# A new order for the head of a fused attention and MLP kernel: mask rows and query low part first, values by slot, adjacent banks, and 91 matmuls of a constant

## The chip, the cores and the metric

The kernel runs on one core of a Trainium2 chip. The metric is the device time of one execution in microseconds, as the median of several runs; lower is better.

## What is computed

Attention with a block-sparse mask, followed by a gated MLP. There are 4 batches, 8 heads, 768 positions of 64 values; the mask works on blocks of 32 positions, with three random blocks a row that come as an input.

```python
scores = scale * np.matmul(q, k.transpose(0, 1, 3, 2))
# mask: neighbours, first and last block row and column, and for each qb the blocks sampled_blocks[qb]
scores = np.where(mask, scores, -1000000000.0)
scores = scores - np.max(scores, axis=-1, keepdims=True)
attn = np.exp(scores)
attn = attn / (np.sum(attn, axis=-1, keepdims=True) + 1e-09)
x = np.matmul(attn, v).transpose(0, 2, 1, 3).reshape(B * S, H * D)   # 3072 x 512
h = x @ w_in                                                          # 512 -> 2048
return (h * np.clip(h + 3.0, 0.0, 6.0) / 6.0) @ w_out                 # 2048 -> 512
```

## The kernel before

The attention is cut into 64 units of one batch, one half of the query positions (384) and one head, u0 to u63. The MLP is cut into 64 steps, m0 to m63: for each batch and half, eight steps of 256 hidden columns. The 32 weight blocks w0 to w31 come as 64-bit floats; ACT (`size`) and DVE (`bits_0` to `bits_2`, `low`) turn each into a high and a low part of 32 bits. The mask is prepared once (k0).

All instructions are issued in an order that is written out by hand: a string, SCORE, names one step after another (`u0 s_0` is the first score pair of unit 0). A step that is named early does first what it needs. Each engine works through its own queue in that order, and so does SP, which issues every load and store.

A unit goes through these steps. `loadq`, `loadk`, `loadv` load; `qh` and `kh` round query and key on ACT; `ql` writes the query's low part on DVE, `kl` the key's on POOL; `qb` copies the query below the mask rows. `m_0` to `m_2` are matmuls for the row maxima, two of 384 columns each, `r_0` to `r_2` the maxima over blocks of 32 on DVE, `fin` adds the block mask `mq` and takes the maximum. `mt` turns it by a matmul with the unit matrix (units 0 to 9) or by a DMA (from 10 on), `qm` copies it into the row of `qb` on ACT. `s_0` to `s_2` are the scores, four matmuls each (`QA,KA` and `qb,kb`), `e_0` to `e_2` the exps on ACT, `av` the product with the values. `uc`, `dw` or `tt`, `uu` empty it; `rg`, `rc`, `rs`, `rb` spread the denominators over partitions by DMA and back; `ux` scales. The MLP's `h_` matmuls need the scaled heads of half a row of units, `ga` to `gl` are the gate, `o_` the second product.

PSUM has eight banks: two tiles `big` of two banks, one `av`, and three single tiles `out0` to `out2` for the MLP's result. Units 1 to 8, which come before the MLP starts, use two of the `out` banks for their maxima, in turn. Units 0 to 11 are wide: their value tile holds, for each of six chunks, 64 columns of values and 64 of ones. The later ones use the two 64-column parts as two slots.

Of the kernel before, what the change touches and what calls it, by code (L numbers as in the profile page):

```python
# [20 lines left out]
P = 128  # L21
# [21 lines left out]
    ql; w2 size; k0 kb_0; u0 m_0; u1 loadq; w0 size; u0 m_1 r_0; k0 indc; u0 r_1 m_2; k0 kb_1; u0 kl r_2; k0 rows mq
    qb_11; u1 qh; w2 bits_0; u1 loadk qb; w2 bits_1; k0 qb_01 identc mqc qb_10; u0 fin_0 fin_1; k0 qb_00; w2 bits_2;
    u0 mt qm; w0 bits_0; w1 load; w2 high; u0 s_0; w0 bits_1; u0 s_1; w2 low; u0 e_0; u1 ql; w2 save; u0 e_1 s_2; w0
    bits_2; u2 loadq; u0 av_0; u1 kh; w3 load; w0 high; u1 kl m_0; u0 e_2 av_1; u1 r_0; w1 size; w0 low; u2 loadk; u1
    m_1; u0 av_2; w1 bits_0; u2 qh; w0 save; w1 bits_1; u2 qb ql; w3 size; u2 loadv; w1 bits_2; u3 loadq; u0 dw; u1
    r_1; w5 load; w1 high; u0 uc; w1 low; u1 m_2; u2 kh; u1 r_2; w1 save; u2 kl m_0 r_0; u3 loadk; u1 fin_0; u2 m_1;
    w5 size; u1 fin_1; w3 bits_0; u1 mt; u2 r_1; u1 qm s_0; w5 bits_0; u1 s_1 e_0; w5 bits_1; u2 m_2; w5 bits_2; u1
    e_1 s_2; u2 r_2; w4 load; u1 av_0; w5 high; u1 e_2; u2 fin_0 fin_1; u1 av_1; w5 low; u3 kh; w3 bits_1; w5 save; u3  # L50
    qh; u1 av_2; w3 bits_2; u3 qb ql; w3 high; w6 load; u2 mt; u3 kl; u4 loadq; u3 m_0; u1 dw; u3 loadv r_0; u2 qm; u1
    uc; u2 s_0; w4 size; u1 rg; w3 low; u2 s_1 e_0; u4 loadk; w4 bits_0; u3 m_1; w3 save; w4 bits_1; u2 e_1; m1
    loadout_0; u2 s_2; u3 r_1; u2 av_0; w6 size; u2 e_2; w6 bits_0; w4 bits_2; u3 m_2; u4 qh; u2 av_1; u3 r_2; w8
    load; w4 high; u4 qb; u2 av_2; u1 rc; u4 ql; u1 rs; u4 kh; u3 fin_0; u5 loadq; u3 fin_1; u4 kl m_0; u2 dw; u4
    loadv; u3 mt; u4 r_0; u3 qm; u2 uc; u3 s_0; w6 bits_1; u5 loadk; u3 s_1; w8 size; w6 bits_2; u4 m_1; u3 e_0; w8
    bits_0; w7 load; u1 rb; u4 r_1; w6 high; u3 s_2 e_1 av_0; w6 low; u3 e_2; w4 low; w6 save; u4 m_2; u5 qh; w8
    bits_1; w4 save; u3 av_1; u5 kh ql; u4 r_2; u5 qb; u6 loadq; u5 kl; u3 av_2; w7 size; u5 m_0; u3 dw; u5 loadv r_0;
    u6 loadk; u3 uc rg; u1 ux_0; u5 m_1; m1 loadin_0; u4 fin_0; u1 ux_1; u4 fin_1; m1 loadin_1; u5 r_1; u4 mt qm s_0;
    u1 ux_2; w8 bits_2; u4 s_1 e_0; w7 bits_0; w10 load; u5 m_2; w8 high; w7 bits_1; u4 s_2 e_1; u3 rc; u4 av_0; u5
    r_2; u3 rs; u6 kh; u5 fin_0; u4 av_1; u5 fin_1; u4 e_2; u6 kl qh; u4 av_2; u6 qb; w10 size; u6 ql; u7 loadk; u5  # L60
    mt; w7 bits_2; u7 loadq; u6 m_0; u4 dw; u5 qm; u6 r_0; w9 load; u6 loadv; w7 high; u5 s_0; u3 rb; w8 low; u4 uc;
    u5 s_1 e_0; w7 low; w8 save; u6 m_1; u5 e_1 s_2; w10 bits_0; w7 save; u6 r_1; u5 av_0 e_2; w10 bits_1; u7 kh; u6
    m_2; w10 bits_2; u5 av_1; u7 qh; u6 r_2; u7 kl; w11 load; w10 high; u5 av_2; u7 qb; m1 loadout_1; w9 size; u3
    ux_0; u8 loadk; u5 uc; u7 loadv; u6 fin_0 fin_1; u3 ux_1; u7 ql; u6 mt; u5 dw; u3 ux_2; u7 m_0; u8 loadq; u6 qm;
    u5 rg; w9 bits_0; u6 s_0; w11 size; u7 r_0; u6 s_1 e_0; w9 bits_1; u7 m_1; u6 e_1 s_2; w9 bits_2; u6 av_0; u7 r_1;
    w12 load; w9 high; u6 e_2; w9 low; u7 m_2; u8 kh; u6 av_1; u5 rc; w9 save; u7 r_2; u5 rs; u8 qh kl qb; u6 av_2; u7
    fin_0; u6 uc; u8 loadv; u7 fin_1; u8 ql; u9 loadk; u7 mt; u6 dw; w10 low; u8 m_0; u9 loadq; u7 qm; w12 size; u7
    s_0; u8 r_0; u5 rb; u7 s_1 e_0; w12 bits_0; w10 save; u8 m_1; w11 bits_0; u7 e_1 s_2; w11 bits_1; u7 av_0; u8 r_1;
    u7 e_2; u9 kh; w11 bits_2; u8 m_2; u7 av_1; w12 bits_1; w14 load; w11 high; u8 r_2; u9 kl qh; u7 av_2; u9 qb; u8
    fin_0; u7 uc; u9 loadv; u8 fin_1; u10 loadk; u5 ux_0; u8 mt; u7 dw; u9 ql; u8 qm; u7 rg; w12 bits_2; u5 ux_1; u9  # L70
    m_0; u10 loadq; u8 s_0; w14 size; u5 ux_2; w13 load; w12 high; u9 r_0; u8 e_0; w14 bits_0; u8 s_1; w14 bits_1; u8
    s_2 e_1; w14 bits_2; u8 av_0 e_2; w11 low; w15 load; u7 rc; w14 high; w12 low; u7 rs; u9 m_1; w11 save; u9 m_2;
    u10 kh; u9 r_1; w12 save; u8 av_1; u10 qh kl; u9 r_2; u10 qb; u8 av_2; w13 size; u9 fin_0 fin_1; u8 uc; u10 loadv;
    w14 low; u9 mt; u8 dw; u7 rb; w13 bits_0; u9 qm; w13 bits_1; w14 save; w15 size; u9 s_0; u11 loadk; w13 bits_2; u9
    s_1 e_0; w15 bits_0; w16 load; u10 ql; w13 high; u9 s_2; w15 bits_1; u11 loadq; u9 e_1 av_0; w13 low; u9 e_2; w15
    bits_2; w13 save; u9 av_1; u7 ux_0; w15 high; w18 load; u7 ux_1; w15 low; u10 m_0; u11 kh; u10 m_1; u7 ux_2; w15
    save; u9 av_2; u10 r_0; u11 qh kl qb; u10 r_1 m_2; w16 size; u11 loadv; u9 uc; u10 r_2; m0 h_00; u12 loadk; u9 dw;
    w18 size; u9 rg; w16 bits_0; m0 h_10; u10 fin_0 fin_1; w18 bits_0; u10 mt; m0 h_01; w16 bits_1 bits_2; m0 h_11; m2
    loadin_0; w18 bits_1; w16 high; w17 load; m1 h_00; w18 bits_2; m0 ga; m2 loadin_1; u11 ql; w19 load; m1 h_10; w18
    high; u9 rc; u12 loadq; m0 gb; u9 rs; m1 h_01; w18 low; m0 gh; w16 low; w18 save; u10 s_0; m3 loadin_0; m0 gl; w16  # L80
    save; w17 size; m1 h_11; u10 e_0; m3 loadin_1; w19 size; u10 s_1; w17 bits_0; u9 rb; m1 ga; w17 bits_1; m0 o_00;
    w19 bits_0; m0 o_01; u10 e_1; w17 bits_2; m0 o_10; w19 bits_1; w17 high; w20 load; u10 s_2; w19 bits_2; m0 o_20;
    u10 e_2; w17 low; w22 load; u10 av_0; m2 loadout_0; m1 gb; w19 high; w17 save; u12 kh; u9 ux_0; u11 m_0 m_1; u12
    qh; w19 low; m0 o_11; u9 ux_1; u11 r_0; u12 kl; w19 save; m0 o_21; u12 qb; m1 gh; u10 av_1; u11 r_1; m2 loadout_1;
    w22 size; m1 gl; u13 loadk; u11 m_2; w20 size; u10 av_2; u11 r_2; u9 ux_2; m2 h_00; u10 uc; u12 loadv; w22 bits_0;
    u14 loadv; u10 dw; u11 fin_0; m2 h_10; u11 fin_1; w22 bits_1; u11 mt; w22 bits_2; m2 h_01; u12 ql; w22 high; w24
    load; m2 h_11; w20 bits_0; u13 loadq; m4 loadin_0; w22 low; u12 m_0; w20 bits_1; w22 save; m2 ga; m1 o_00; m4
    loadin_1; u12 r_0; m1 o_01; m2 gb; m1 o_10; u12 m_1; w20 bits_2; m2 gh; u12 m_2; m1 o_20; u12 r_1; w21 load; w20
    high; m2 gl; m1 o_11; m3 loadout_0; w24 size; u12 r_2; u11 s_0; m1 o_21; w24 bits_0; u11 e_0; u12 fin_0; u11 s_1;
    u12 fin_1; m3 loadout_1; w24 bits_1; u12 mt; u11 s_2 e_1; w24 bits_2; u11 av_0 e_2; w20 low; w23 load; w20 save;  # L90
    w24 high; m2 o_00; u13 kh; w24 low; m2 o_01; w24 save; u13 qh kl; u12 s_0; u13 qb; u12 s_1; w21 size; u11 av_1;
    u12 e_0; u13 ql; u14 loadk; u12 e_1; w21 bits_0; u14 loadq; u13 m_0; w21 bits_1; u11 av_2; w23 size; u13 r_0 m_1;
    w23 bits_0; u11 uc; u13 loadv m_2; u12 suma; u15 loadv; u11 dw; m2 o_10; u11 rg; m2 o_20; u13 r_1; m2 o_11; m4
    loadout_0; u13 r_2; u12 s_2; u13 fin_0; m3 h_00; u13 fin_1; u12 e_2; w23 bits_1; u13 mt; w23 bits_2; u14 kh; m3
    h_10; u12 sumb; w26 load; w23 high; u12 av; u14 qh; u11 rc; u14 kl; u11 rs; u14 qb; u13 s_0; u12 tt sumc; u15
    loadk; u16 loadv; m3 h_01; u12 uu; u13 e_0; u14 ql; u13 s_1; w26 size; w23 low; u15 loadq; m5 loadin_0; m3 h_11;
# [826 lines left out]
```

## Time and profile before

| | before |
|---|---|
| median of 3 runs | 998.83 us (998.39 to 999.71) |
| the profiled execution | 998.31 us, span 996.5 us |
| PE busy | 954.3 us, 96% of the span |
| DVE, ACT, POOL busy | 649.4, 468.2, 248.8 us |
| mean granted clock of PE | 0.990 |
| DMA | 155.48 MB in 136981 packets, 72755 of them under 512 B |

PE carries the span, so its gaps and its clock are read first, stage by stage. A row of the stage table gives a stretch, each engine's busy time in it with the count of its instructions, the granted clock, the share of the DMA engines and the rate. A row in order of time gives start, duration, engine, line, operation and tiles, and in brackets how long the engine was idle before it and what ended that. Since nearly all instructions go through one helper, their line says nothing; the tile names do.

### The profile page before, as it was taken

The page shows a single profiled execution, that of the slowest core. Times are in us where ns is not written, and L with a number is a line of the kernel's source. Part 1 is how long each engine was busy: PE and PEld are TensorE (multiplying, and loading weights), DVE is VectorE, ACT ScalarE, POOL GpSimd, SP SyncE. Part 2 cuts the span into 40 slices and gives each one's busy share as a digit, 9 for nine tenths or more (in the row PEclk, how much of TensorE's full clock was granted, in tenths as well). Part 3 has the DMA queues.
Part 4 walks back from the last instruction along what each step waited for, and adds up shares of the span by engine and source line. Part 5 has one row for each costly group of instructions (what it writes and reads, how often), then busy time and mean ns, then how long its engine had stood idle before and what let it go on. Part 6 is the DMA issues. An engine that isn't in the chain of part 4 may idle for free.

```text
span 996.5 us, 13217 instructions
## 1 busy us (share of the span) xinstructions
PE 954.3 (96%) x4750; PEld 772.0 (77%) x4750; DVE 649.4 (65%) x924; ACT 468.2 (47%) x712; POOL 248.8 (25%) x148
## 2 busy tenths in 40 slices
PE   5888889999999999999999999999999999999998
...
PEclk9799799999999999999999999999999999999999
...
GB/s 183 188 224 210 222 264 217 216 224 182 149 153 138 136 121 172 149 132 140 162 139 132 96 165 158 136 126 154 159 114 140 128 149 183 103 78 141 161 122 74
DMA packets 136981, 155.48 MB, mean 156 GB/s; under 512 B 72755, under 2 KB 85171, under 8 KB 136916
## 3 DMA queue, kind: packets, MB, share of 16 engines
...
q8 instruction: 37, 0.61, 0.3%
...
## 4 chain that ended last, share of the span: by engine, by line
PE 83%; DVE 6%; ACT 4%; issue 3%; DMA 3%; POOL 0%; SPq 0%; DVEq 0%; ACTq 0%; POOLq 0%
PE big L356 46%; PE out L356 24%; PE av L356 13%; DVE acc L356 2%; DVE bm L356 2%; DMA wraw<-w_out 1%; ACT pr L356 1%; ACT qb L356 1%; DMA wout_lo<-xhl 1%; DVE xhl L356 1%; DVE QA L356 1%; ACT rec L356 0%; DMA qb<-mneg 0%; ACT g L356 0%; DMA spread<-rec 0%
## 5 line engine op out<-in xcount | busy, mean ns | idle before, releaser
L356 PE MATMUL big<-xhl,win_hi 128*128 128x384 f32 x1024 | 264.0, 339 | 2.7 <-DVE bm L356 2.1
L356 POOL TENSOR_TENSOR glo<-g,ghi 128x768 fp32r<-128x768 f32 x64 | 118.7, 1855 | 477.2 <-ACT ghi L356 456.8
L356 DVE TENSOR_REDUCE bm<-big 128x24 f32<-128x768 f32 x168 | 158.6, 954 | 82.0 <-PE big L356 80.8
L356 ACT ACTIVATE pr<-big 128x768 f32<-128x768 f32 x192 | 152.0, 812 | 123.6 <-PE big L356 123.0
L356 PEld LDWEIGHTS big<-xhl,win_hi 128*128 128x128 f32 x1024 | 185.5, 188 | 14.5 <-DVE bm L356 6.0
L356 POOL TENSOR_TENSOR kb<-kraw,KA 64x768 fp32r<-64x768 f32 x64 | 124.7, 1948 | 254.5 <-ACT KA L356 208.2
L356 PE MATMUL big<-xhl,wlo_in 128*128 128x384 f32 x512 | 173.1, 338 | 0.0
L356 PE MATMUL av<-pr,vo 128*64 128x384 f32 (+1 forms) x768 | 166.1, 498 | 0.0
L356 PE MATMUL out<-wout_hi,ghi 128*128 128x512 f32 x384 | 152.8, 398 | 0.0
L356 PE MATMUL out<-wout_hi,glo 128*128 128x512 f32 x384 | 151.7, 395 | 0.0
L356 PE MATMUL out<-wlo_out,ghi 128*128 128x512 f32 x384 | 150.7, 392 | 0.0
L356 PE MATMUL big<-QA,KA 128*128 128x384 f32 x384 | 139.3, 363 | 5.9 <-ACT pr L356 2.8
L356 PE MATMUL big<-qb,kb 97*128 97x384 f32 x384 | 135.0, 352 | 8.9 <-ACT qb L356 7.7
L356 ACT ACTIVATE g<-big,half_b 128x768 f32<-128x768 f32 x64 | 57.7, 902 | 159.7 <-PE big L356 145.9
L356 DVE SCALAR_TENSOR_TENSOR g<-g,big 128x768 f32<-128x768 f32 x64 | 60.8, 949 | 95.1 <-ACT g L356 94.8
L356 PEld LDWEIGHTS av<-pr,vo 128*64 128x64 f32 (+1 forms) x768 | 69.2, 149 | 65.6 <-issue 50.9
L356 PE MATMUL big<-KA,QA 128*128 128x384 f32 x336 | 93.8, 370 | 12.5 <-DVE QA L356 10.4
L356 DVE TENSOR_TENSOR acc<-pr 128x768 f32<-128x768 f32 x52 | 57.9, 1113 | 69.3 <-ACT pr L356 69.2
L356 PEld LDWEIGHTS big<-KA,QA 128*128 128x128 f32 x336 | 75.6, 255 | 33.6 <-issue 13.3
L356 PEld LDWEIGHTS big<-xhl,wlo_in 128*128 128x128 f32 x512 | 96.1, 188 | 0.3 <-DMA wlo_in<-win_lo 0.3
L356 PEld LDWEIGHTS big<-QA,KA 128*128 128x128 f32 x384 | 74.9, 195 | 27.2 <-ACT pr L356 8.4
L356 ACT CAST ghi<-g 128x768 fp32r<-128x768 f32 x64 | 53.3, 833 | 79.4 <-DVE g L356 54.0
...
## 6 DMA issues: line engine op xcount, KB each, us to landing
...
```

What stands on the lines that cost most here:

```text
L356: return lambda *a, **k: tc.keep_in_program_order(op(*a, **k))
```

## The change

Five things. First, the opening: query and key of unit 0 are loaded first, the mask's rows `krows` (tile `pr`) and the unit matrix ahead of the first weights; the query's low part is computed ahead of the mask; the mask's step `allow` is cut into four; the block mask `mq` is multiplied from the plain F32 copy of `krows`.

Second, the two value slots lie behind each other (slot, chunk, column) from unit 12 on, where they were interleaved (chunk, slot, column).

Third, the three `out` banks are one tile OUT. The early maxima always use its first two banks, and one reduce reads both.

Fourth, `warm` steps: a tile of ones is filled on POOL as the first thing, and 91 matmuls of 384 columns multiply it with itself into the third bank of OUT. Nothing reads their result. SCORE has them at 21 places between the opening and unit 9's maxima; the last digit of the name is the count.

Fifth, SCORE has a new order up to the first MLP steps, and some exchanges of neighbours in stretches behind them.

```diff
+    OUT = outp.tile([P, NT, DM], F32, name="out")
-    VO = [const.tile([P, NC, 2, D], F32, name=f"vo{side}") for side in range(2)]
+    VO = [const.tile([P, 2 * NC * D], F32, name=f"vo{side}") for side in range(2)]
...
+        def heat(self):
+            self.hot = sb.tile([P, 2, HALF], F32R, name="ghi")
+            nc.gpsimd.memset(self.hot.bitcast(F32), 1.0)
+
+        def warm(self, *number):
+            for _ in range(number[-1]):
+                pe.matmul(OUT[:, 2, :HALF], lhsT=self.hot[:, 0, :P], rhs=self.hot[:, 1], start=True, stop=True)
...
         def mq(self):
-            self.mqp = big_tile()
+            self.mqp = OUT[:, 2]
             for t in range(NC):
-                pe.matmul(self.mqp[:, 0, t * NB:(t + 1) * NB], lhsT=self.ind_r[...], rhs=self.mval[:, 64:88], start=True, stop=True)
+                pe.matmul(self.mqp[:, t * NB:(t + 1) * NB], lhsT=self.ind_f[...], rhs=self.mval[:, 64:88].bitcast(F32), start=True, stop=True)
...
         def loadv(self):
-            self.vo = VO[self.side]
-            self.vv = self.vo[:, :, self.side if self.wide else self.n // 2 % 2]
+            if self.wide:
+                self.vo = VO[self.side].rearrange("p (c a d) -> p c a d", a=2, d=D)
+                self.vv = self.vo[:, :, self.side]
+            else:
+                self.vv = VO[self.side].rearrange("p (a c d) -> p a c d", a=2, d=D)[:, self.n // 2 % 2]
...
         def m(self, t):
             if self.early:
-                bank = (self.n - 1) // 2
-                ps = [outp.tile([P, DM], F32, name=f"out{(bank + 1 + j) % NT}")[:, :HALF] for j in range(2)]
+                ps = OUT[:, 0:2]
...
         def r(self, t):
-            if self.early:
-                for j in range(2):
-                    dve.tensor_reduce(out=bm[:, j], in_=self.mps[t][j].rearrange("p (n e) -> p n e", e=BLK), axis=AX.X, op=ALU.max)
-            else:
-                dve.tensor_reduce(out=bm, in_=self.mps[t].rearrange("p j (n e) -> p j n e", e=BLK), axis=AX.X, op=ALU.max)
+            dve.tensor_reduce(out=bm, in_=self.mps[t].rearrange("p j (n e) -> p j n e", e=BLK), axis=AX.X, op=ALU.max)
...
-    k0 samp; u0 loadq loadk; k0 table; w0 load; w2 load; k0 ind index; u0 loadv; u1 loadv; k0 ident allow; u0 qh qb kh
+    u0 loadq loadk; k0 samp table ind; u1 loadv; k0 ident; u0 loadv; w0 load; w2 load; u0 qh qb ql kh; k0 index; u1
```

What stands in the queues now, at three places. First SP's opening, the loads in their order (`samp` and `tab` are the mask's inputs, `wraw` a weight block), before:

```order
L356 DMA samp<-sampled 24x6
L356 DMA qraw<-qT 128x384
L356 DMA kraw<-kT 128x768
L356 DMA tab<-table 24x48
L356 DMA wraw<-w_in 128x1024 x2
L356 DMA pr<-krows 33x768
L356 DMA vo_119<-vP 128x6x64
L356 DMA vo_120<-vP 128x6x64
L356 DMA tmp<-ident 128x128
```

and now:

```order
L358 DMA qraw<-qT 128x384
L358 DMA kraw<-kT 128x768
L358 DMA samp<-sampled 24x6
L358 DMA tab<-table 24x48
L358 DMA pr<-krows 33x768
L358 DMA vo_121<-vP 128x6x64
L358 DMA tmp<-ident 128x128
L358 DMA vo_120<-vP 128x6x64
L358 DMA wraw<-w_in 128x1024 x2
```

The query and key went to the top, and the two weight loads moved behind five others.

Second, DVE from the mask's last row to unit 0's `fin` (`bm<-bm,mq`), before:

```order
L356 TENSOR_SCALAR mval<-tab 24x24
L356 SCALAR_TENSOR_TENSOR QA<-qraw,QA 64x384
L356 TENSOR_REDUCE bm<-big 128x24 x3
L356 TENSOR_SCALAR xhl<-xhl 128x512
L356 SCALAR_TENSOR_TENSOR xhl<-wraw,xhl 128x512
L356 COPY mq<-big 128x144
L356 TENSOR_TENSOR bm<-bm,mq 128x72
```

and now:

```order
L358 TENSOR_SCALAR mval<-tab 24x24
L358 TENSOR_REDUCE bm<-big 128x24 x2
L358 COPY mq<-out 128x144
L358 TENSOR_REDUCE bm<-big 128x24
L358 TENSOR_SCALAR xhl<-xhl 128x512
L358 SCALAR_TENSOR_TENSOR xhl<-wraw,xhl 128x512
L358 TENSOR_TENSOR bm<-bm,mq 128x72
```

The low part (`QA<-qraw,QA`) has left this place; it is now DVE's first instruction. The two weight steps stay ahead of `fin`.

Third, PE from the first product of values of unit 7 to unit 8's first scores, before (`big<-ident,mneg` is unit 8's `mt`, `big<-KA,QA` unit 9's maxima):

```order
L356 MATMUL av<-pr,vo_120 128x384 x2
L356 MATMUL out_911<-KA,QA 128x384
L356 MATMUL out_912<-KA,QA 128x384
L356 MATMUL av<-pr,vo_120 128x384 x4
L356 MATMUL big<-ident,mneg_117 2x128 x3
L356 MATMUL big<-KA,QA 128x384 x2
L356 MATMUL big<-QA,KA 128x384
```

and now, from unit 8's last maximum on (`out<-ghi` are the constants):

```order
L358 MATMUL out<-KA,QA 128x384 x2
L358 MATMUL big<-KA,QA 128x384 x4
L358 MATMUL out<-ghi 128x384 x2
L358 MATMUL big<-KA,QA 128x384 x2
L358 MATMUL out<-ghi 128x384 x16
L358 MATMUL big<-ident,mneg_117 2x128 x3
L358 MATMUL out<-ghi 128x384
L358 MATMUL big<-QA,KA 128x384
```

All three maxima of unit 9 and 19 constants stand ahead of unit 8's scores now, where it was one maximum.

More of the change, by code (lines that the diff above doesn't have):

```diff
@@ L41 @@
 SCORE = """
-    k0 samp; u0 loadq loadk; k0 table; w0 load; w2 load; k0 ind index; u0 loadv; u1 loadv; k0 ident allow; u0 qh qb kh
[L43 to L96, printed above, removed]
@@ new lines @@
+    r_1; k0 warm_101; u1 s_0; w5 bits_1; u1 s_1 e_0; w5 bits_2; u2 m_2; u1 e_1 s_2; w3 bits_2; w4 load; u2 r_2; u1
+    av_0; w5 high; w6 load; u1 e_2; u2 fin_0 fin_1; u1 av_1; w5 low; u3 kh; w5 save; u3 qh kl; u1 av_2; u3 qb; w3
+    high; u2 mt; u1 dw; u3 loadv ql; u4 loadk; u2 qm; w3 low; k0 warm_111; u3 m_0; u4 loadq; u1 uc; u2 s_0; u3 r_0; w3
+    save; w4 size; u1 rg; u2 s_1 e_0; w4 bits_0; m1 loadout_0; u3 m_1; w4 bits_1; u2 e_1 s_2; u3 r_1; u2 av_0; w6
+    size; w4 bits_2; u2 e_2; w6 bits_0; u3 m_2; w8 load; u4 qh; u2 av_1; w6 bits_1; w4 high; u3 r_2; u4 qb; u2 av_2;
@@ new lines @@
+    e_0; u1 ux_2; u5 m_2; w8 bits_2; u4 e_1 s_2; w7 bits_0; w10 load; u4 av_0; w8 high; w7 bits_1; u4 e_2; u5 r_2; u4
+    av_1; u6 qh; u3 rc; u6 qb; u5 fin_0; u3 rs; u5 fin_1; u6 kh ql; u4 av_2; w7 bits_2; u7 loadq; w8 low; w7 high; w9
+    load; u5 mt; u6 m_0 loadv; u4 dw; w7 low; w8 save; w10 size; u6 kl r_0; w7 save; u5 qm; u4 uc; k0 warm_147; u5
+    s_0; u3 rb; u5 s_1; w10 bits_0; u5 e_0; w10 bits_1; u7 loadk; u6 m_1; u5 e_1 s_2; u6 r_1; u5 av_0; w9 size; w10
+    bits_2; u5 e_2; m1 loadout_1; w9 bits_0; w11 load; u6 m_2; u7 qh; w9 bits_1; u5 av_1; w10 high; u6 r_2; u7 qb; u5
@@ new lines @@
+    av_2; u3 ux_0; u7 kh; u6 fin_0 fin_1; u7 ql; u6 mt; u5 uc; u7 loadv; w9 bits_2; u7 m_0; u8 loadq; u3 ux_1; u7 kl
+    r_0; u5 dw; w12 load; u6 qm; u5 rg; k0 warm_154; u7 m_1; w11 size; u6 s_0; u7 r_1; w9 high; u8 loadk; u6 s_1 e_0;
+    u3 ux_2; u7 m_2; w9 low; u6 e_1 s_2; u7 r_2; w9 save; u6 av_0 e_2; u7 fin_0 fin_1; u8 qh; w10 low; u6 av_1; u8 qb;
+    u5 rc; w10 save; w12 size; u8 ql; u5 rs; u6 av_2; w11 bits_0; u9 loadq; u8 kh; w12 bits_0; w11 bits_1; u7 mt; u8
+    m_0; u6 uc; u8 loadv; w11 bits_2; u6 dw; u8 kl r_0; w14 load; u7 qm; w11 high; k0 warm_164; u7 s_0 s_1 e_0; w12
@@ new lines @@
+    bits_1; u9 loadk; u8 m_1; u5 rb; u7 e_1; w12 bits_2; u7 s_2; u8 r_1; w13 load; u7 av_0; w12 high; u7 e_2; w11 low;
+    u7 av_1; u9 qh; w12 low; w11 save; u9 qb ql; w12 save; w14 size; u7 av_2; u10 loadq; w14 bits_0; u9 kh; w14
+    bits_1; u8 m_2; u9 loadv; u7 uc; u5 ux_0; u9 m_0 m_1; u7 dw; u9 kl r_0; u5 ux_1; u7 rg; w13 size; u8 r_2; k0
+    warm_172; u9 m_2; u5 ux_2; u10 loadk; u8 fin_0 fin_1; w14 bits_2; u9 r_1; w14 high; w15 load; u9 r_2; k0 warm_189
+    warm_197; u8 mt qm; k0 warm_201; u8 s_0; u7 rc; u9 fin_0; u7 rs; u9 fin_1; u8 s_1; w14 low; u8 e_0; w13 bits_0;
@@ new lines @@
+    w14 save; u8 e_1 s_2; w13 bits_1; u8 av_0; w13 bits_2; u10 kh; w16 load; u8 e_2; u10 kl; u8 av_1; u10 qh qb; u7
+    rb; u9 mt; u8 av_2; w15 size; u10 ql; u11 loadk; u9 qm; w15 bits_0; u11 loadq; w13 high; w15 bits_1; u9 s_0; u10
+    loadv; u8 uc; w13 low; u9 s_1 e_0; w15 bits_2; w13 save; u8 dw; u9 s_2; w18 load; w15 high; u9 av_0 e_1; w15 low;
+    u7 ux_0; w15 save; u9 e_2 av_1; u7 ux_1; u11 kh; u7 ux_2; u10 m_0 m_1 r_0; u9 av_2; u11 qh kl qb; u10 r_1; w16
+    size; u10 m_2; u11 loadv; u9 uc; m0 h_00; u10 r_2; u12 loadk; u9 dw; w18 size; u9 rg; w16 bits_0; m0 h_10; u10
@@ new lines @@
+    w22 load; u10 e_2; m1 gb; w17 save; m0 o_21; u12 kh; u11 m_0; w19 low; m2 loadout_1; u11 m_1; u10 av_0; u12 qh;
+    u11 r_0; w19 save; u12 kl qb; u11 r_1; m1 gh; u10 av_1; w20 size; u9 ux_0; u13 loadk; u12 ql; u11 m_2; w22 size;
+    u10 av_2; m1 gl; u13 loadq; u11 r_2; u9 ux_1; m2 h_00; u10 uc; u12 loadv; u14 loadv; w22 bits_0; u10 dw; m2 h_10;
+    w22 bits_1; u9 ux_2; m2 h_01; w22 bits_2; u11 fin_0; w22 high; w24 load; m2 h_11; u11 fin_1; m4 loadin_0; w20
+    bits_0; u11 mt; w22 low; u12 m_0; m2 ga; m4 loadin_1; w20 bits_1; m1 o_00; w22 save; u12 r_0; m1 o_01 o_10; m2 gb;
@@ new lines @@
+    u12 m_1; w20 bits_2; u12 m_2; m2 gh; m1 o_20; u12 r_1; w21 load; w20 high; m2 gl; m1 o_11; m3 loadout_0; w24 size;
+    u12 r_2; u11 s_0; m1 o_21; u11 e_0; w24 bits_0; u12 fin_0; u11 s_1; u12 fin_1; m3 loadout_1; w24 bits_1; u12 mt;
+    u11 s_2 e_1; w24 bits_2; m2 o_00; w20 low; w23 load; w24 high; m2 o_01; u11 e_2; w24 low; w20 save; u11 av_0; w24
+    save; u13 kh qh kl; u11 av_1; u13 qb; w21 size; u12 s_0; u13 ql; u14 loadk; u12 s_1 e_0; w21 bits_0; u14 loadq;
+    u11 av_2; w21 bits_1; u12 e_1; w21 bits_2; w23 size; u13 m_0; u12 suma; w26 load; u13 m_1; u11 uc; u13 loadv; m2
@@ new lines @@
+    o_10; u15 loadv; u11 dw; u13 r_0; m2 o_20; w21 high; u11 rg; w23 bits_0; u13 m_2; m4 loadout_0; u13 r_1; m2 o_11
+    o_21; u13 r_2; u12 s_2; m4 loadout_1; u13 fin_0 fin_1; m3 h_00; w23 bits_1; u12 e_2; u13 mt; w23 bits_2; u14 kh;
+    m3 h_10; u12 sumb; w28 load; w23 high; u12 av; u14 qh; u11 rc; u14 kl; u11 rs; u14 qb; w26 size; u13 s_0; u12
+    sumc; u15 loadk; u12 tt; u16 loadv; u14 ql; m3 h_01; u13 e_0; u12 uu; u15 loadq; w23 low; u13 s_1; m5 loadin_0;
+    w26 bits_0; w23 save; m3 h_11; u13 e_1; w26 bits_1; u11 rb; w26 bits_2; u13 s_2; m3 ga; m5 loadin_1; u13 suma; w30
@@ new lines @@
+    e_0; u15 fin_0 fin_1; w26 low; u15 mt; m4 o_00; u14 e_1; w26 save; u14 s_2; u11 ux_1; u14 suma; m4 o_10; u14 e_2;
+    u11 ux_2; m5 h_00; u16 kh; u14 sumb; m5 h_10; u16 qh; u14 sumc; u16 qb ql; u15 s_0; w30 size; u16 kl; u17 loadq;
+    m5 h_01; w25 size; m6 loadin_1; u15 e_0; m5 h_11; m7 loadin_0; w30 bits_0; u17 loadk; w25 bits_0; u15 s_1; m5 ga;
+    w25 bits_1; u14 av; w25 bits_2; u15 e_1; m5 gb; w27 load; w25 high low; m5 gh; u15 s_2; u18 loadv; u15 suma; u14
+    tt; w25 save; u16 m_0; u15 e_2; m4 o_20; m5 gl; u16 r_0; u17 kh; m4 o_01; u14 uu; u16 m_1; u17 qh; u16 m_2; u17
@@ L411, in fused_kernel @@
         NEEDS = {
-            "indc": "ind", "identc": "ident", "kb_0": "ind", "kb_1": "ind", "index": "samp", "allow": "index table", "mq": "allow indc", "rows": "allow indc", "mqc": "mq",
+            "index": "samp", "allow_0": "index table", "allow_1": "allow_0", "allow_2": "allow_1", "allow_3": "allow_2",
+            "mq": "allow_3 ind", "rows": "allow_3 indc", "indc": "ind", "mqc": "mq", "identc": "ident", "kb_0": "ind", "kb_1": "ind",
             "qb_00": "rows", "qb_01": "rows", "qb_10": "rows", "qb_11": "rows",
@@ L447, in index, with allow @@
             dve.tensor_copy(out=self.idxf, in_=self.sampled[:, 0:6:2])
-        def allow(self):
-            self.mval = const.tile([NB, 88], F32R, name="mval")
-            nc.gpsimd.memset(self.mval.bitcast(F32), 0.0)
+        def allow(self, j):
             msk = self.tab[:, 1]
-            for j in range(3):
+            if j == 0:
+                self.mval = const.tile([NB, 88], F32R, name="mval")
+                nc.gpsimd.memset(self.mval.bitcast(F32), 0.0)
+            if j < 3:
                 eq = sb.tile([NB, NB], F32, name="eq")
```

477 lines of the change are left out of this document (245 added, 232 removed).

## Prediction, made before the changed kernel ran

> **What bounds the kernel now.** I read first the page's slices, then one table of busy time by stage, then PE's rows of the first 140 us in order of time with what ended each gap, and last the chain of waits for the same stretch. The profiled execution took 998.31 us, a span of 996.5 and 1.8 around it; the median of the runs shown is 998.83, 0.5 above it. The sum below is made against 998.31.
>
> ```profile
> PE   5888889999999999999999999999999999999998
> PEclk9799799999999999999999999999999999999999
> ```
>
> PE is full from the seventh slice on. What is open lies in the first five or six slices, and the granted clock dips there too. The stages, with engine busy time in the order PE, PEld, DVE, ACT, POOL, then clock, DMA share and GB/s:
>
> ```profile
> 0.00:121.00 121.00, 95.38 (x345) 68.46 (x345) 91.71 (x172) 82.86 (x136) 27.85 (x32) 0.92 0.66 206
> ...
> 28.50:39.50 11.00, 8.57 (x25) 6.91 (x26) 7.73 (x18) 4.61 (x8) 1.81 (x1) 0.54 0.52 160
> 39.50:99.50 60.00, 52.44 (x217) 36.94 (x215) 51.92 (x97) 47.44 (x80) 12.85 (x7) 1.00 0.70 216
> 99.50:107.00 7.50, 6.48 (x17) 5.10 (x17) 4.27 (x9) 5.59 (x10) 1.22 (x1) 0.54 0.83 283
> ...
> 113.80:117.50 3.70, 3.70 (x9) 2.42 (x8) 3.16 (x6) 2.68 (x6) 0.00 (x0) 0.54 0.87 277
> ...
> 136.00:996.50 860.50, 846.51 (x4341) 692.02 (x4340) 546.18 (x733) 376.74 (x564) 218.95 (x115) 1.00 0.50 148
> ```
>
> The head, 0 to 121 us, ends with the first MLP matmul. In it PE is idle for 25.6 us and at about half clock for 22; behind 136 us it is busy for 98.4% and any lead won in the head is carried to the end as it stands. Inside the head no engine is full: from 39.5 to 99.5 PE and DVE have 52 of 60 us each, so units are paced by hand-overs between two nearly full queues.
>
> ```profile
> 7.56 1.62 PE L356 MATMUL big<-KA,QA 128*128 128x384 f32 x4 [7.56 <-DVE QA L356]
> ...
> 18.18 0.52 PE L356 MATMUL big<-qb,kb 97*128 97x384 f32 x1
> 18.50 0.52 PE L356 MATMUL big<-QA,KA 128*128 128x384 f32 x1
> ...
> 27.22 0.98 PE L356 MATMUL out<-KA,QA 128*128 128x384 f32 x2 [1.45 <-DVE bm L356]
> ...
> 33.89 0.66 PE L356 MATMUL big<-qb,kb 97*128 97x384 f32 x1 [1.84 <-ACT qb L356]
> ...
> 43.92 0.41 PE L356 MATMUL big<-qb,kb 97*128 97x384 f32 x1 [0.61 <-ACT qb L356]
> 44.17 0.34 PE L356 MATMUL big<-QA,KA 128*128 128x384 f32 x1
> 44.34 0.34 PE L356 MATMUL big<-qb,kb 97*128 97x384 f32 x1
> ...
> 89.98 0.41 PE L356 MATMUL big<-qb,kb 97*128 97x384 f32 x1 [0.74 <-ACT qb L356]
> ...
> 100.69 0.69 PE L356 MATMUL big<-QA,KA 128*128 128x384 f32 x1 [1.02 <-DVE bm L356]
> ...
> 111.81 0.41 PE L356 MATMUL big<-qb,kb 97*128 97x384 f32 x1 [1.52 <-ACT qb L356]
> ...
> 135.76 0.44 PE L356 MATMUL big<-QA,KA 128*128 128x384 f32 x1 [2.60 <-ACT pr L356]
> ```
>
> Three things to see. The matmuls of 384 columns start 0.32 us apart at 18 us and about 0.175 apart at 44: PE runs at half speed in its first stage too, although the clock column says 1.00 there. Unit 1 has its first scores at 33.89, 17 us behind unit 0, while units 2 to 7 follow each other by 9.2 (43.92 to 89.98, five steps). And the gaps that precede the dips are short: 1.45, 1.02 and 1.52 us.
>
> **The start.** In order of time, all engines:
>
> ```profile
> 0.75 0.43 SPq L356 DMA_DIRECT2D samp<-sampled  x1
> ...
> 1.24 0.37 SPq L356 DMA_DIRECT2D qraw<-qT  x1
> ...
> 2.56 0.81 SPq L356 DMA_DIRECT2D wraw<-w_in  x2
> ...
> 4.78 0.83 ACT L356 CAST KA<-kraw 128x768 fp32r<-128x768 f32 x1
> ...
> 6.66 0.17 DVE L356 TENSOR_SCALAR mval<-tab 24x24 fp32r<-24x24 f32 x1
> 6.86 0.56 DVE L356 SCALAR_TENSOR_TENSOR QA<-qraw,QA 64x384 fp32r<-64x384 f32 x1
> ...
> 8.58 1.82 DVE L356 TENSOR_REDUCE bm<-big 128x24 f32<-128x768 f32 x2 [1.16 <-PE big L356]
> ...
> 9.68 1.23 ACT L356 ACTIVATE xhl<-wraw 128x512 f32<-128x512 f32 x2 [4.06 <-DMA wraw<-w_in]
> ...
> 14.49 1.22 ACT L356 CAST qb<-big 24x384 fp32r<-24x384 f32 x3
> ...
> 16.01 0.67 ACT L356 CAST qb<-big 1x384 fp32r<-1x384 f32 x1 [0.30 <-PE big L356]
> ```
>
> The low part of the query now stands ahead of the mask work on DVE, and its load is issued 0.5 us earlier; the first maxima then wait for KA alone, which ends near 5.2 instead of 5.6, so they start about 2.3 us sooner. DVE reads them once the mask row (mval, end 6.83) is out: 1.7 us sooner than 8.58. Against this the two weight loads go behind krows, both values and ident, 547 KB. At the 206 GB/s of the head that is 2.6 us, at the 283 of a dense stage 1.9; I take 2.1, so the second weight lands at 11.8. Its size step (0.62) and then six ACT rows (four casts of 0.41, two of about 0.5) stand ahead of the unit's qb: 15.1 instead of 16.01. Both ways of loading leave between 0.3 and 2.3; I take **0.9**. On DVE two weight steps (0.5 and 0.7) stand between the last maximum and fin; they end near 13.5 and are hidden by that ACT row.
>
> **The clock in the first stage.** 25 constants come ahead of unit 0's mt: ten while PE would be empty until 5.2 (4 us at 0.32 each is 3.2), fifteen while it waits for the maxima (2.6 to 4.8 us in a gap of some 4). If PE is warm by then, its 12 score matmuls gain 0.14 each, **1.7**. Most of it reaches unit 1 through the exps: its first maxima and the size step of the next weight.
>
> **Unit 1.** The chain of waits has a load here:
>
> ```profile
> 27.12 5.25 DMA wraw<-w_out
> 32.40 0.66 ACT xhl L356
> 33.08 0.68 ACT qb L356
> ```
>
> The load needs a buffer that DVE frees with the last bit step of weight 1. Before, that step stands behind unit 2's low part; now the three bit steps stand together right behind unit 1's first maximum. With exps 0.9 + 1.7 earlier less what ACT's casts take up (KA, win_hi in between; I walk the rows to a size step 1.3 sooner), the step ends near 23.8, 2.9 before the load's 27.12. ACT still waits for that load ahead of unit 1's qb, so the 2.9 goes through one for one: unit 1's scores at 31.0. So start and clock together are worth **2.9** here, not 0.9 + 1.7. Twelve score matmuls of unit 1 without the dip of 28.5 give again **1.7**.
>
> **Early maxima.** 48 reduces of half a bank pair become 24 of both:
>
> ```profile
> L356 DVE TENSOR_REDUCE bm<-big 128x24 f32<-128x768 f32 x168 | 158.6, 954 | 82.0 <-PE big L356 80.8
> ...
> L356 DVE TENSOR_REDUCE bm<-out 128x12 f32<-128x384 f32 x48 | 24.4, 551 | 8.4 <-PE out L356 8.1
> ```
>
> Two of 551 against one of 954 is 0.15 each, 3.6 on DVE in all. Against it, the next maximum's first matmul waits for the whole reduce, up to 0.4 more; 16 such successions would cost 6.4. PE waited only four times for such a reduce:
>
> ```profile
> PE out L356 <- DVE bm L356: 2.8, 4, 1.4
> ...
> ACT rec L356 <- DMA vo<-vP: 3.1, 1, 3.1
> ```
>
> Between units PE waits for ACT's qb, not for DVE, so I take **0.5** of a range from -6.4 to +3.6.
>
> **Units 8 and 9.** At clock 0.54 the stages from 99.5 and 113.8 lose 0.46 of 11.2 us, 5.1. Four, then eighteen constants stand there. DVE and ACT carry part of that stretch, so I take three quarters, **3.8**.
>
> **The price of the constants.** The trace has none; the nearest rows are the 384-column matmuls, 0.175 warm and 0.32 cold. 91 are 16 to 29 us. The cover is the 25.6 us of idle PE; where it is missed, each costs its 0.175 and whatever stands behind it in PE's queue. The groups stand ahead of mt, scores or maxima that waited in the rows above, but by places chosen beforehand. I take **0.5** lost, ends 0 and 16.
>
> **Edits at nothing.** Values by slot: 52 loads in six times longer pieces, the same bytes; the row above has one wait of 3.1 on a value load, so 0 to 3.1, and 0 because they are issued a unit ahead. The mask product in plain F32 is six matmuls of 24 columns in the wait for maxima; before they took 1.3 and up to that again would be hidden by two reduces of 0.95. The last fence of PE rows has a stop of 2.60 at 135.76 for an exp behind a weight load on ACT; the new order lets the MLP's Relu pass first but leaves the exp behind that load, so 0, with 2.6 as the end. The late shuffles keep the PE queue full: 0.
>
> Sum: 2.9 + 1.7 + 0.5 + 3.8 - 0.5 = **8.4**, 998.31 - 8.4 = 989.9. I say 990.0.
>
> **A rule against it.** The Trainium skill, "TensorE: Matmul & The Clock Gate", Part 1 and its closing table, says that the array starts throttled, is released after some 3.4 us of sustained work and falls back after an idle window of that length, so that no gap over about 3 us is to be left. The start agrees (0.32 at 18 us). The dips don't: gaps were 1.0 to 1.5, and the 2.6 at 135.76 brought none. By the rule the dips would not come from those gaps, and filling them would not cure them; the second rival below is that case, from rows.
>
> **The rivals.** *Slower, the constants lie on the path* (0.12): none of the waits comes where its group stands, and PE holds ready matmuls back. All 91 at 0.175 against the other terms' 8.9: 998.3 - 8.9 + 15.9 = 1005. It decides from 51 uncovered constants on. For it: 16 us have to fit 25.6 us of idle that is cut into waits of 0.6 to 1.8; against it: more than half of the constants stand at the three long waits.
>
> *The dips stay* (0.15): DVE and ACT leave PE's queue as thin as before between groups and the clock still falls at 28, 99 and 114. Then only 2.9 + 0.5 - 0.5 is left: 995.4. For it: the dips came at 40 to 70% busy PE, without a long gap.
>
> *Nothing is won* (0.10): the head is carried by DVE, 91.7 of 121 us, and unit 8 now stands behind four more weights' bit steps and unit 9's maxima; the lead is given back before 121. 998, within a microsecond or two.
>
> *More* (0.15): DVE's 3.6, the whole 5.1, the 2.6 at 135.76 and the start's other end, 1.4 more, come through: 8.4 + 3.1 + 1.3 + 2.6 + 1.4 less 1 for what overlaps, 982.5.
>
> **How the numbers follow.** My forecast has 0.48 and its own range of 986 to 993.5. Over 0.2%, 2 us, is what a measurement of this kernel tells from no change. Faster: 0.48 + 0.15 + 0.15 = 0.78; same 0.10; slower 0.12. The range takes in the dips that stay and the deeper case and leaves out the slower rival and half of the unchanged one: 981.5 to 997.5.
>
> **What would show it.** Right: first maxima near 5.2, unit 0's scores 0.17 apart, unit 1's first scores near 31, no clock under 0.9 in the slices behind the first unit, the first MLP matmul near 112.5, and 98% PE behind it. Wrong, if PE's head holds constants while a qb or a maximum is already done, if the dips return, or if the rows behind 136 us lose what the head won.

## The result: slower, and the profile after

The changed kernel took 1012.7 us, the median of its runs (1007.8 to 1015.0), against 998.6 for the kernel before: a ratio of 1.0127, 95% interval 1.0097 to 1.0157. The forecast was 990.0, at most 997.5. The profiled execution is the fastest of its four runs, 1007.78 us with a span of 1006.0.

The slices of the page of the changed kernel, PE's busy tenths and the granted clock, and then two stages of it (PE, PEld, DVE, ACT, POOL, clock, DMA share, GB/s); the head now ends at 126:

```profile
PE   8888899999999999999999999999999999999997
PEclk9999999999999999999999999999999999999999
```

```profile
0.00:126.00 126.00, 105.61 (x442) 82.11 (x443) 92.39 (x149) 83.66 (x137) 29.33 (x33) 0.96 0.65 198
...
136.00:1006.00 870.00, 849.43 (x4351) 693.71 (x4349) 550.01 (x738) 378.83 (x567) 220.82 (x115) 1.00 0.49 147
```

PE looks fuller in the first slices, as intended: 105.6 us busy in the head instead of 95.4. It is full of the wrong thing. The head has become 5 us longer, and the stage from 136 us to the end 9.5 longer: the head's delay and some 4.5 of its own.

PE's own list of waits, in the changed kernel (who waited for whom, us in all, times, longest):

```profile
PE out L358 <- DVE bm L358: 14.5, 10, 2.5
PE big L358 <- DVE QA L358: 4.3, 3, 2.0
PE out L358 <- DVE wraw L358: 3.7, 5, 1.0
```

The first row was 2.8 us in 4 times before, the third is new. What stands behind them are these rows of PE in order of time:

```profile
20.52 0.69 PE L358 MATMUL out<-KA,QA 128*128 128x384 f32 x2
21.04 1.45 PE L358 MATMUL av<-pr,vo 128*128 128x384 f32 x4
24.48 2.01 PE L358 MATMUL out<-ghi 128*128 128x384 f32 x10 [1.99 <-DVE bm L358]
26.33 0.52 PE L358 MATMUL out<-KA,QA 128*128 128x384 f32 x2
27.90 2.18 PE L358 MATMUL out<-ghi 128*128 128x384 f32 x11 [1.05 <-DVE bm L358]
...
72.10 1.49 PE L358 MATMUL out<-ghi 128*128 128x384 f32 x7 [2.49 <-DVE bm L358]
...
94.43 0.96 PE L358 MATMUL out<-ghi 128*128 128x384 f32 x4 [2.17 <-DVE bm L358]
...
106.85 0.62 PE L358 MATMUL out<-ghi 128*128 128x384 f32 x2 [2.52 <-DVE bm L358]
```

The rows `out<-ghi` are the constants. All ten waits of the 14.5 us stand in front of a group of them (1.99, 1.05, 1.05, 0.87, 0.87, 0.44, 2.49, 1.05, 2.17, 2.52), none in front of a maximum. A constant reads a tile of ones and writes the third bank, which nothing else uses at this point; it has nothing to wait for. Yet DVE's rows show what released it:

```profile
23.47 0.96 DVE L358 TENSOR_REDUCE bm<-out 128x24 f32<-128x768 f32 x1
...
26.89 0.96 DVE L358 TENSOR_REDUCE bm<-out 128x24 f32<-128x768 f32 x1 [0.67 <-PE out L358]
```

The reduce that starts at 23.47 ends at 24.43 and the ten constants start at 24.48; the reduce that starts at 26.89 ends at 27.85 and the next eleven start at 27.90. The constants were to fill PE's wait for a reduce. Instead they sit that wait out and begin when the next real matmul could: the maximum at 26.33 was free to start at 24.4, as its buffer was read by then. The reason can be read in the program itself, in what each PE instruction waits for; the rows of the changed kernel around 24 us are these (`waits DVE_49` is a wait for a count that DVE raises):

```
36 L358 MATMUL av<-pr,vo_120 128x384
37 L358 MATMUL out<-ghi 128x384 [waits DVE_49]
38 L358 MATMUL out<-ghi 128x384 x9
39 L358 MATMUL out<-KA,QA 128x384 x2
40 L358 MATMUL out<-ghi 128x384 [waits DVE_49]
```

The edit that gave the maxima adjacent banks made the three banks one allocation, `OUT`. In the program built from it a write to the third bank is ordered behind a read of the first two. Only the first constant of a group carries the wait, and the maximum behind these ten carries none.

The landmarks, from the starts of PE's rows (first qb matmul of a unit, first MLP matmul) and the page:

| us | before | after |
|---|---|---|
| first maximum | 7.56 | 5.17 |
| unit 0's scores | 16.73 | 15.18 |
| unit 1's | 33.89 | 34.65 |
| unit 4's | 63.85 | 62.52 |
| unit 7's | 89.98 | 95.45 |
| unit 8's | 98.97 | 111.63 |
| first MLP matmul | 120.96 | 125.88 |
| span | 996.5 | 1006.0 |

The opening won what was forecast, the lead was eaten in the middle of the head, and the MLP lost on from +4.9 to +9.5.

### The profile page after: what moved, and what is told of

It is laid out like the page before. It is cut to its first block, busy times and chain, and to the rows that moved or that the text cites. A ratio compares the mean times of both kernels' runs of the same rounds, so it can differ in the third digit from the quotient of the medians.

```text
span 1006.0 us, 13404 instructions
## 1 busy us (share of the span) xinstructions
PE 965.0 (96%) x4847; PEld 785.7 (78%) x4847; DVE 650.1 (65%) x900; ACT 468.5 (47%) x712; POOL 252.2 (25%) x149
## 4 chain that ended last, share of the span: by engine, by line
PE 81%; DVE 10%; issue 3%; ACT 3%; DMA 2%; SPq 0%; DVEq 0%; ACTq 0%
PE big L358 44%; PE out L358 27%; PE av L358 11%; DVE bm L358 3%; DVE acc L358 3%; DVE xhl L358 2%; ACT pr L358 1%; DVE QA L358 1%; DVE uu L358 1%; DMA wraw<-w_out 1%; DVE wraw L358 0%; DMA wlo_in<-win_lo 0%; DVE g L358 0%; DMA wraw<-w_in 0%; ACT xhl L358 0%
## 5 line engine op out<-in xcount | busy, mean ns | idle before, releaser
L358 PE MATMUL av<-pr,vo 128*64 128x384 f32 (+1 forms) x768 | 162.1, 493 | 0.0
L358 PE MATMUL big<-qb,kb 97*128 97x384 f32 x384 | 132.0, 344 | 1.4 <-ACT qb L358 1.4
L358 PEld LDWEIGHTS av<-pr,vo 128*64 128x64 f32 (+1 forms) x768 | 67.0, 146 | 64.8 <-issue 47.7
```

What stands on the lines that cost most here:

```text
L358: return lambda *a, **k: tc.keep_in_program_order(op(*a, **k))
```

## Experiments

Five theories. (1) The one allocation makes false waits, and with them the constants lie on the path. (2) The new order itself is slower. (3) The constants are too many even without a false wait. (4) The joined allocation costs without the constants too. (5, from the prediction) Values by slot are worth nothing. All ratios are to the kernel before, run in the same set, with 95% intervals; its median was 998.6 in the set of the first four runs below, 998.8 in the next four and 999.6 in the last four.

To part the clock from the rest I use one derived number: over a kernel's runs, the mean of time times (1 - granted clock), its clock loss. Before it is 8.4 us (35 runs; 8.8 and 9.4 in the other two sets), in the changed kernel 9.4 (4 runs). What is left, 990.0 and 1002.7, I call the time at full clock. The clock is given to 0.001, so each run's loss is good to about half a microsecond. The name promises more than it holds: over 222 runs, those of each kernel and set about their own mean, a microsecond of clock loss goes with about 0.8 us of time and not with 1.

**The third bank apart.** Of the changed kernel,

```
-    OUT = outp.tile([P, NT, DM], F32, name="out")
+    OUT = outp.tile([P, 2, DM], F32, name="out")
+    OUT2 = outp.tile([P, DM], F32, name="out2")
```

with the constants, the mask's product and the third output in `OUT2`. Nothing is added, removed or reordered.

> The changed kernel with one edit: the third bank is an allocation of its own (OUT2), OUT keeps the first two. The instructions, their order and their banks stay. Theory 1 (the constants lie on the path because a write to bank 3 waits for the reduce that reads banks 1 and 2 of the same allocation): the rows of the constants lose their waits for DVE's maxima (14.5 us in the changed kernel's profile), the first MLP matmul comes at 113 to 120 instead of 125.9, the time is 992 to 1000. Theory 2 (the new order itself is slower, whatever the constants do): first MLP matmul at 124 or later, 1008 to 1014. Theory 3 (the constants are too many even without the false wait, since the waits they were put into are shorter than they): the waits go, the first MLP matmul at 120 to 124, 1002 to 1008.

Measured: 996.8 us, ratio 0.9971 (0.9953 to 0.9989), 16 us below the changed kernel. The first MLP matmul came at 116.98. PE's rows of the same place, and the row of the waits that was 14.5:

```profile
22.91 1.45 PE L358 MATMUL av<-pr,vo 128*128 128x384 f32 x4
23.91 2.19 PE L358 MATMUL out<-ghi 128*128 128x384 f32 x10
26.35 0.68 PE L358 MATMUL out<-KA,QA 128*128 128x384 f32 x2 [0.25 <-DVE bm L358]
26.87 2.07 PE L358 MATMUL out<-ghi 128*128 128x384 f32 x11
29.10 0.66 PE L358 MATMUL out<-KA,QA 128*128 128x384 f32 x2 [0.15 <-DVE bm L358]
29.59 0.86 PE L358 MATMUL out<-ghi 128*128 128x384 f32 x4
30.81 0.68 PE L358 MATMUL out<-KA,QA 128*128 128x384 f32 x2 [0.35 <-DVE bm L358]
```

```profile
PE out L358 <- DVE bm L358: 1.0, 4, 0.4
```

Now the constants run right behind the av matmuls, and each following maximum still waits 0.15 to 0.35 for its reduce: the groups fit their waits almost exactly. In the program of this run the constants carry no wait, and the same count of DVE stands at the maximum behind them. Theory 1 holds.

The Trainium skill, "PSUM — Partial Sum Buffer", section on bank collisions, says to guard PSUM with semaphores by bank and group of 32 partitions, and that engines on different banks run clean. This run's trace agrees as to the banks: eleven constants write the third bank from 26.87 to 28.94 while DVE's reduce that starts at 28.00 and takes 0.95 reads the other two. The wait across the banks, with what it costs in the MLP (below), was worth 16 us.

**No constants, one allocation.** All `warm` entries of the order taken out.

> The changed kernel without its 91 constants; order, joined allocation and joined reduces stay. Theory 1 (constants on the path through the false wait): no later than the kernel before by the head, first MLP matmul at 115 to 121, 994 to 1001, with clock dips as many as before or more. Theory 2 (the order is slower): 1006 to 1013. Theory 3 (too many constants): like theory 1, and below the kernel with the bank split off.

Measured: 1001.8 us, 1.004 (1.0021 to 1.0059), first MLP matmul at 119.13. Just above the range of theory 1 and far below that of theory 2; theory 3, by which it would lie below the 996.8 of the run above, falls. The constants cost 11 us in the changed kernel, but a loss remains that they don't explain.

**The order of before, with the changed kernel's code and no constants.**

> The changed kernel's code (one allocation for the three banks, joined reduces of the early maxima, values by slot, the mask's small products in F32) with the order of the kernel before and no constants. Theory 1 and 3: within 0.4% of before, 995 to 1002. Theory 2 (only the new order costs): 998, within 0.2% of before. Theory 4 (the joined reduce or the one allocation costs, by later maxima in the head and by waits at the block switches, 3.7 us in the changed profile): 1002 to 1008, with waits of the MLP's output matmuls for the copies of the block before.

Measured: 1001.8 us, 1.0037 (1.0018 to 1.0056): as slow as the new order in the run above. Theory 2 falls. The time lies at the edge between theories 1 and 4. This profile too has the row `PE out <- DVE wraw` with 3.7 us in 5 times, which theory 4 named; the next run parts the two.

**No constants, third bank apart.**

> The changed kernel without its constants and with the third bank an allocation of its own. Against the run without constants it shows what the one allocation costs apart from the constants (the mask's product, and the first matmul of a new block into a bank that the copies of the block before still read): theory 1 and 3, no difference beyond 0.2%, 994 to 1001; theory 4 (the allocation slows the block switches): 3 us less than without constants alone.

Measured: 997.8 us, 0.9992 (0.9975 to 1.001), 4 less than with one allocation. The stage from the first MLP matmul to the end took 875.8 us here, 879.6 with one allocation and 875.5 in the kernel before. Where those 4 are lost is seen in the MLP of the changed kernel. At four of the seven switches to a new block, and at the end, the output matmuls waited for DVE's copies; the first and the last of the five such rows, and the last copies on DVE:

```profile
259.12 0.50 PE L358 MATMUL out<-wout_hi,ghi 128*128 128x512 f32 x1 [1.03 <-DVE wraw L358]
...
999.22 0.50 PE L358 MATMUL out<-wout_hi,ghi 128*128 128x512 f32 x1 [0.78 <-DVE wraw L358]
```

```profile
998.48 0.69 DVE L358 COPY wraw<-out 128x512 f32<-128x512 f32 x1 [7.84 <-PE out L358]
1001.63 1.29 DVE L358 COPY wraw<-out 128x512 f32<-128x512 f32 x2 [2.46 <-PE out L358]
```

The copy of the first finished bank waits until PE pauses in the others, and PE then waits for the copy. In the kernel before, the copy ran beside the matmuls:

```profile
990.05 0.69 DVE L356 COPY wraw<-out 128x512 f32<-128x512 f32 x1 [5.04 <-PE out L356]
990.08 0.39 PE L356 MATMUL out<-wlo_out,ghi 128*128 128x512 f32 x1
990.31 0.40 PE L356 MATMUL out<-wout_hi,glo 128*128 128x512 f32 x1
```

**Three allocations of one bank.** All false waits gone; early maxima again as two reduces, always in banks one and two, constants in the third:

```
+    OUT = [outp.tile([P, DM], F32, name=f"out{t}") for t in range(NT)]
-                ps = OUT[:, 0:2]
+                ps = [OUT[j][:, :HALF] for j in range(2)]
```

> The changed kernel (order, constants, values by slot as they are) with three allocations of one bank each: early maxima in the first two with a reduce for each bank, constants in the third, output matmuls in all three. Theory 1 (one allocation makes false waits: of the constants on the reduces in the head, of output matmuls on the copies at block switches, of the first copy on later output matmuls at the end): below the run with only the third bank split off (996.8) by the 1.6 us that its last step still takes longer than in the kernel before, and by what its first two banks cost at block switches, so 993 to 996. Theory 4 (the joined reduce is worth its 0.5 us): 0.5 of that goes back, 994 to 996. Rival (the rest of the loss behind the head comes from the order between 720 and 800 us): no better than 996.8, the end as before.

Measured: 992.9 us, 0.9936 (0.9911 to 0.996): 20 us below the changed kernel, and the fastest median but one of the study. Its own rows at the forecast's landmarks:

```profile
31.08 0.41 PE L358 MATMUL big<-qb,kb 97*128 97x384 f32 x1 [0.45 <-ACT qb L358]
...
116.02 0.61 PE L358 MATMUL big<-xhl,win_hi 128*128 128x384 f32 x2
```

**A joined pair in the head, three banks from the first output matmul on.** The pool of the pair and the single bank is closed there and another opened.

> The changed kernel with a pair and a single bank for the head and, from the first output matmul on, three single banks in their place. Theory 1: as with three single banks, 993 to 996, and below it by up to 1 us if the joined reduce gains anything; above it by up to 2 us if the change of allocation makes the first output matmuls wait.

Measured: 993.9 us, 0.9954 (0.9933 to 0.9975). Not to be told from the run above: joined reduces gain nothing that shows.

**The same, with the order of before behind the head.**

> As the run before it, and behind the last matmul into h of the first MLP step the remaining operations stand in the order of the kernel before. If the new order loses 2 to 3 us between 720 and 800 us (as the steps of the runs with the new order show and the run with the old order does not), the time is 990 to 993.5. If that loss comes from the earlier start itself (the transfers of weights and units then collide), it stays, and the time is 993 to 997.

Measured: 993.75 us, 0.9946 (0.9931 to 0.9962). No gain. By the starts of POOL's `glo` rows, one for each MLP step (times are those of the kernel before), this run's lead over the kernel before is 6.7 us up to step 44 at 765 us and 4.2 from step 47 at 819 on; with the new order (the run before this one) it falls from 8.4 at 723 to 6.0 at 740 and 5.7 at 784, and is 7.1 at 819. Each order has a place where some of the lead goes. The first of the two expectations is refuted; what takes the microseconds there was not settled.

**The order of before, no constants, same banks.**

> The order of the kernel before and no constants, with a joined pair for the early maxima, the mask's product in a bank of its own, values by slot, and three single banks from the first output matmul on. What the joined reduce, adjacent banks and values by slot are worth without the false waits: 996 to 999 if nothing or the 0.5 us forecast; 1001 or more if the wait of a maximum for the whole reduce of the pair is what made the old order slower with one allocation (1001.8).

Measured: 997.7 us, 0.9997 (0.9978 to 1.0016): joined reduces, adjacent banks, values by slot and the F32 mask product together are worth nothing that shows once no wait is false.

**Which constants pay.** Three banks, and then no constants, only the 65 from unit 1 on, and only the 26 of the opening.

> The kernel with three allocations of one bank (992.9, product of time and granted clock 988.5 on the mean of its runs) without any of the 91 constants. If the constants pay when nothing holds them back (they bring the granted clock up in the head): slower, 994.5 to 997, with 8 to 11 us of clock loss instead of 3.5 and a product of 984 to 986. If they cost as much as they bring: 992 to 993.5. The bound of the prediction that all of them lie on the path (16 us) would give 982 or less.

> The kernel with three allocations of one bank, with the 65 constants from unit 1 on and without the 26 of the opening (10 ahead of the first maximum, 15 ahead of unit 0's row of maxima, 1 before its scores). The opening's constants are followed by a half clock near 9 to 16 us in the profiles and 15 of them stand ahead of the row of maxima: if they cost more than they save, 990.5 to 992.5; if it is they that keep the clock up at 27 to 38, 994 to 996.

> The kernel with three allocations of one bank, with the 26 constants of the opening and without the 65 from unit 1 on. If the gain of clock comes from the later ones (dips at 27 to 38 and 100 to 110): 994 to 997, like without any; if the opening's constants alone carry it: 992 to 993.5.

| constants | median us | ratio | clock loss | time at full clock |
|---|---|---|---|---|
| none | 994.1 | 0.9956 (0.9939 to 0.9973) | 9.1 | 985.4 |
| 26 in the opening | 994.8 | 0.9957 (0.9938 to 0.9976) | 10.7 | 984.2 |
| 65 from unit 1 on | 993.6 | 0.994 (0.9917 to 0.9963) | 2.0 | 991.3 |
| all 91 | 992.9 | 0.9936 (0.9911 to 0.996) | 3.5 | 988.5 |

The new order alone is worth 3.6 us: 994.1 against the 997.7 of the run above, no constants in either.

The granted clock is raised by the later constants, as expected. The time says less. By means, to which the last two columns add up, all 91 win 2.5 us and the 65 later ones 1.2; by medians it is 1.2 and 0.5, and the intervals overlap. The first row's set of runs is not that of the last row, but with the third bank apart, in one set, the sign is the same (996.8 with the constants, 997.8 without). So they are worth some 1 to 2 us, not proven, where the column of the clock shows 5.6 to 7.1. If all 91 lay on the path, the run without them would have been at 982 or below; so they neither lie on it all nor come free. The time without any is just under the range for constants that pay, and the run with the later ones alone falls between its two ranges. Two stages of the run without any, and of the run with all, show what the later ones do to the clock (the columns as above):

```profile
20.00:40.00 20.00, 15.93 (x47) 11.11 (x46) 14.84 (x30) 11.37 (x20) 4.88 (x3) 0.74 0.55 190
100.00:120.00 20.00, 16.71 (x60) 12.14 (x59) 12.97 (x24) 13.86 (x22) 3.32 (x2) 0.83 0.58 186
```

```profile
20.00:40.00 20.00, 19.10 (x87) 14.75 (x86) 17.69 (x33) 13.48 (x23) 5.30 (x3) 1.00 0.68 216
100.00:120.00 20.00, 19.35 (x89) 14.67 (x88) 15.08 (x27) 15.55 (x26) 3.64 (x2) 1.00 0.63 201
```

Two things keep the last two columns from being gain and price. One is the 0.8 from above. The other is that the granted clock does not show the cold opening: without constants unit 0's scores start 0.32 us apart, half speed, in a stage whose clock stands at 1.00, so part of that kernel's loss is counted as time at full clock.

```profile
0.00:20.00 20.00, 11.67 (x37) 9.16 (x38) 9.97 (x23) 11.20 (x18) 7.58 (x22) 1.00 0.64 203
...
14.01 0.48 PE L366 MATMUL big<-ident,mneg 128*2 128x128 f32 x3 [2.61 <-DVE mneg L366]
...
16.29 0.52 PE L366 MATMUL big<-qb,kb 97*128 97x384 f32 x1
16.61 0.52 PE L366 MATMUL big<-QA,KA 128*128 128x384 f32 x1
```

With all 91 the same scores start about 0.18 apart. But there the turn of unit 0's maxima (`big<-ident,mneg`) comes 1 us later, right behind the fifteen constants and without a wait of its own:

```profile
10.22 4.97 PE L358 MATMUL out<-ghi 128*128 128x384 f32 x15
15.02 0.35 PE L358 MATMUL big<-ident,mneg 128*2 128x128 f32 x3
...
16.64 0.34 PE L358 MATMUL big<-qb,kb 97*128 97x384 f32 x1
16.82 0.34 PE L358 MATMUL big<-QA,KA 128*128 128x384 f32 x1
```

So the constants of the opening do warm PE up, and in this profile they lie on the path by about 1 us and give most of it back; in time they win nothing (994.8 against 994.1).

**Values as before.** Three banks and all constants, the two heads' columns side by side chunk by chunk again.

> The kernel with three allocations of one bank, with the values stored as in the kernel before, the two heads' columns side by side chunk by chunk (so twice the DMA packets under 512 B). If values by slot are worth nothing, as forecast: 992 to 994, within 0.2%. If the shorter DMAs (2.9 us instead of 3.3) matter: 1 to 3 us slower, 994 to 996.

Measured: 992.0 us, 0.9932 (0.9907 to 0.9957). Values by slot are worth nothing.

## Why the prediction was wrong, step by step

**The price of the constants** is the step that failed. It took 0.5 us because the groups stand where PE waited before. The places were well chosen: with the bank apart, the waits there shrank to 0.15 to 0.35 us. What it missed is that the changed code gave the constants something to wait for. The prediction priced the joined banks as a matter of reduces alone and never asked who else writes into the allocation that the three banks had become. The slower rival saw the outcome, constants in PE's queue ahead of ready matmuls, and named the sign for it, but reached it through unlucky places and gave it 0.12. Its 1005 charged 15.9 us for the constants and kept the other terms' 8.9 as won. Measured, the kernel without constants stood at 1001.8, with nothing won, and the constants cost 10.9 on top.

**The same allocation in the MLP** was in no term. It is worth 4 us with only the third bank apart, and 3 to 4 more with all three (992.9 against 996.8 with the constants, 994.1 against 997.8 without; 993.9 against 996.8 where only the MLP's banks differ). With the order of before, all of it together is 4.1 (997.7 against 1001.8), so the two parts don't simply add up.

**The start**: right. First maxima at 5.17 (forecast 5.2), unit 0's scores 0.175 apart, its first qb matmul 1.55 sooner. Unit 1's scores at 31.08 with three banks, against 31.0; in the changed kernel 34.65, behind 25 constants that had waited. The first MLP matmul, forecast near 112.5, came at 116.02 with three banks.

**The clock** (1.7 in unit 1, 3.8 in units 8 and 9): right for the granted clock where the constants are free to run, a loss of 3.5 instead of 9.1, so the rival by which the dips stay falls there, though that run's profile keeps some. As time it is too large: the constants' net worth was forecast at 1.7 + 3.8 - 0.5 = 5.0 and measured at 1.2 between medians, 2.5 between means. In the changed kernel not even the clock was won: 9.4 against 8.4. That a constant which waits leaves PE's gap as it was would explain it; no run tests this alone. The changed kernel's profiled run still has dips:

```profile
10.00:20.00 10.00, 9.38 (x40) 7.95 (x40) 6.51 (x12) 8.80 (x17) 2.94 (x3) 0.83 0.57 181
...
30.00:40.00 10.00, 8.08 (x33) 6.82 (x32) 6.53 (x12) 4.33 (x7) 0.04 (x1) 0.83 0.36 123
...
90.00:100.00 10.00, 7.83 (x31) 6.53 (x31) 7.06 (x9) 5.87 (x10) 2.04 (x1) 0.83 0.80 229
```

**Early maxima** at 0.5 of a range from -6.4 to 3.6: nothing measurable, by the pair of 992.9 and 993.9. **Edits at nothing**: right for values by slot, and for the mask product within what the run with the order of before and the banks by stage can tell. **A lead is carried to the end**: roughly. With three banks it is 4.9 us at the first MLP matmul (116.02 against 120.96) and 5.4 at the end of the span (991.1 against 996.5). On the way it grows, and between 720 and 820 us 1 to 3 us of it go in either order.

With all false waits gone the change gives 992.9, 5.9 below before (998.8) and inside the range. The medians split it into 1.1 for the code alone (997.7, inside the noise), 3.6 for the new order and 1.2 for the constants; they come from two sets of runs, so each part is good to about a microsecond. The forecast had 2.9 + 0.5 = 3.4 for the start and the reduces, some of it from warming PE up, and the 5.0 for the constants. So of the 8.4 it is the worth of the constants that falls short even where nothing holds them back.
